# The opening of a transformer block with backward pass: loads in order of need, scores behind the first K and Q, other K and V spread between attention steps

## The chip, the core and the metric

The kernel runs on one core of a Trainium2 chip. A core has five engines that run side by side: TensorE (PE, matmuls), VectorE (DVE), ScalarE (ACT, activations such as exp), GpSimd (POOL) and SyncE (SP, which issues DMA transfers). They synchronise by semaphores. On-chip memory is SBUF (128 partitions); matmuls write to PSUM. The metric is device time in microseconds, the median over runs. A profile is of one execution, so its span can differ a little from the median.

## What is computed

The forward pass of a conditioned transformer block (2048 tokens, width 512, 32 heads of 16, MLP of 1792) and the gradients of all its inputs. The change touches the very beginning: layer norm, modulation by `c`, and Q, K and V of the attention.

```python
mod = (silu(c) @ w_mod).reshape(1, 6, 1, -1)         # sa, ca, ga, sb, cb, gb
h = layernorm(x) * (1 + ca) + sa
q, k, v = split(h @ wqkv)                            # 32 heads of 16
p = softmax(einsum('bhqd,bhkd->bhqk', q, k) * 16 ** -0.5)
x = x + ga * (einsum('bhqk,bhkd->bhqd', p, v) @ wo)
h = layernorm(x) * (1 + cb) + sb
x = x + gb * (relu(h @ w1 + b1) ** 2 @ w2 + b2)
# outputs: x, and the gradients of x, wqkv, wo, w1, b1, w2, b2, c, w_mod for a given grad_out
```

## The kernel before

Heads are worked in quads (`g`, 8 of them), queries in chunks of 512 (`qc`, 4 of them). A *unit* is one chunk of queries with a pair of heads: 64 units, each of `ST` = 16 steps `kb`, one for each block of 128 keys. A step makes scores for two heads (128x1024 in PSUM), ScalarE takes their exponential, and two or more steps later TensorE multiplies it with V ("PV"). In the order of TensorE and SyncE the program's order holds (`manual_schedule`); the other engines' instructions may be reordered when the program is built. So the exponentials of all 64 x 16 = 1024 steps form one stream on ScalarE, and other work ("background": Q and K of later quads, the MLP of earlier chunks) is woven between the steps of TensorE.

```python
KT = kp.tile([P, S], BF16, name="KTq")
first = self.gen_open(Vaug, KT, QTm, stp)
next(first)                                   # opening, first block of 512 tokens
for n, (qc, g, jp) in enumerate(order):       # 64 units
    ...
    for kb in range(ST):                      # 16 steps
        ...
        if n == 0 and kb % 4 == 0:
            next(first, None)                 # a further block of 512 tokens: at kb = 0, 4, 8 (12: the end)
        stt = stp.tile([P, 2, 512], F32, name="st")
        for a in range(2):
            nc.tensor.matmul(stt[:, a, :], lhsT=KT[:, kb * P:(kb + 1) * P], rhs=QTm[2 * jp + a][:], ...)
        pu = pup.tile([P, 2, 512], BF16, name="pu")
        nc.scalar.activation(pu[:], stt[:], ACT.Exp, scale=self.scale)
        ...                                   # PV of earlier steps
        rate = (1.14 if qc else 1.2) if n or kb > 11 else 0
        if rate:
            bg.step(rate)                     # background work
```

`gen_open` is the opening. `DT` = 4 (512 features in tiles of 128), `DH` = 16.

```python
for s4 in range(0, ST, 4):
    nc.sync.dma_start(x0[:, s4:s4 + 4, :], x_v[:, s4:s4 + 4, :])
for t in (1, 0, 2):                           # K, Q, V weights
    nc.scalar.dma_start(wq[:, :, t * D:(t + 1) * D], w_v[:, :, t * D:(t + 1) * D])
for t in (1, 0):                              # weights padded: each head's 16 columns in a field of 32
    nc.vector.memset(wpads[t][:], 0.0)
    for kt in range(DT):
        nc.scalar.copy(wpads[t][:, kt]..., wq[:, kt, t * D:(t + 1) * D]...)
nc.vector.memset(Vaug[:, :, :, DH:DH + 1], 1.0)
self.mod_cols(ps, (0, 1))                     # silu(c) @ w_mod for sa and ca: 32 small matmuls
...
for s4 in range(0, ST, 4):                    # a block: 4 tiles of 128 tokens
    for st in range(s4, s4 + 4):
        nc.vector.bn_stats(stats[:, st, :], x0[:, st, :])
        nc.vector.bn_aggr(mv[:, st, :], stats[:, st, :])
    nc.vector.tensor_scalar(ve[:, b], mv[:, b, 1], EPS, None, ALU.add)
    nc.gpsimd.tensor_tensor(self.rstd1[:, b], ve[:, b], self.mhalf[:], ALU.pow)
    nc.vector.scalar_tensor_tensor(nmr[:, b], ...)
    for st in range(s4, s4 + 4):              # xhat: odd tiles on VectorE, even ones on ScalarE
        ...
    tp = stp.tile([P, DT, 512], BF16, name="st")
    ...                                       # 16 transposes on TensorE
    for kt in range(DT):                      # xm1T = xhat^T * (1 + ca) + sa, VectorE and ScalarE in turn
        ...
    for _ in self.gen_fm(ps, 1, 0, s0, dst=KT[:, s0:s0 + 512]):
        pass                                  # K of quad 0
    if s4 == 0:
        for _ in self.gen_fm(ps, 0, 0, 0, masked=QTm):
            pass                              # Q of quad 0, chunk 0, and its masked copies
    for st in range(s4, s4 + 4):              # V: 4 matmuls a tile, evicted by ScalarE and VectorE in turn
        ...
    if s4 == 0:
        nc.gpsimd.dma_start(self.wmod[:, :, 2 * D:6 * D], wmod_v[:, :, 2 * D:6 * D])
        ...                                   # GpSimd memsets of vpads
    yield 0
```

`gen_fm` is four matmuls of 128x512 into a PSUM tile of the pool `ps` (two buffers, name `pps`), an eviction by VectorE, a store and a DMA transpose. The loads of `c` and of the first third of `w_mod` and the small chain silu(c) (VectorE, ScalarE and again VectorE) are in `phase0`, ahead of this.

Of the kernel before, what the change touches and what calls it, by code (L numbers as in the profile page):

```python
# [104 lines left out]
class K:  # L105
# [70 lines left out]
    def phase0(self):  # L176
# [19 lines left out]
        sb = self.open_pool("modp", bufs=1, side="right")  # L196
        cT_b = sb.tile([P, DT], BF16, name="cT_b")
        with nc.allow_non_contiguous_dma(reason="tiny column-layout load"):
            nc.sync.dma_start(cT_b[:], io["c"].rearrange("o (t p) -> p (o t)", p=P))
        wmod = self.wmod = sb.tile([P, DT, 6 * D], BF16, name="wmod")  # L200
        wmod_v = io["w_mod"].rearrange("(kt p) n -> p kt n", p=P)
        nc.scalar.dma_start(wmod[:, :, 0:2 * D], wmod_v[:, :, 0:2 * D])
        cT = sb.tile([P, DT], F32, name="cT")
        nc.vector.tensor_copy(cT[:], cT_b[:])
# [55 lines left out]
    def phase_fwd(self):  # L260
# [63 lines left out]
        next(first)  # L324
        for n, (qc, g, jp) in enumerate(order):
            if (qc, g, jp) == (1, 0, 0):
                bg.drain()
                self.close_qkv()
                self.open_mlp()
                bg.add(self.gen_weights())  # L330
            accb = accp.tile([P, 512], F32, name="accbank")
            acc = accb[:, 0:8 * (DH + 1)].rearrange("p (a s e) -> p a s e", a=2, s=4)
            self.cur_g = g
            for kb in range(ST):
                if kb == ST // 2 and n + 1 < len(order):
                    if n < 2 * NQ - 1 and jp == 1:
                        bg.until(g + 1)
                    load_q(*order[n + 1])
                    if jp == 1:
                        KTn = load_k(*order[n + 1][:2])  # L340
                if n == 0 and kb % 4 == 0:
                    next(first, None)
                stt = stp.tile([P, 2, 512], F32, name="st")
                for a in range(2):
                    nc.tensor.matmul(stt[:, a, :], lhsT=KT[:, kb * P:(kb + 1) * P], rhs=QTm[2 * jp + a][:],  # L345
                                     start=True, stop=True)
                pu = pup.tile([P, 2, 512], BF16, name="pu")
                nc.scalar.activation(pu[:], stt[:], ACT.Exp, scale=self.scale)  # L348
                u = (n, qc, g, jp, kb, acc, pu)
                now = n * ST + kb  # L350
                pend.extend((u, a, sub) for a in range(2) for sub in range(4))
                rate = (1.14 if qc else 1.2) if n or kb > 11 else 0
                room = int((SPAN - 2 - bg.plan(rate)) / PVT)
                while pend:
                    age = now - (pend[0][0][0] * ST + pend[0][0][4])
                    if age < 2 or (room <= 0 and age < 4):
                        break
                    pv(pend.pop(0))
                    room -= 1
                if rate:  # L360
                    bg.step(rate)
            if jp == 1 and n + 1 < len(order):
                if n < 2 * NQ - 1:
                    bg.until(-(g + 1))
                KT = KTn
# [13 lines left out]
    def gen_open(self, Vaug, KT, QTm, stp):  # L379
# [10 lines left out]
        wpads = self.wpads = [sb.tile([P, DT, NQ, P], BF16, name=f"wpad{t}") for t in range(2)]  # L390
        self.vpads = [sb.tile([P, NQ, 4, 32], BF16, name=f"vpad{i}") for i in range(2)]
        x0 = sa_.tile([P, ST, D], BF16, name="x0")
        x_v = io["A_x"][0].rearrange("(st p) d -> p st d", p=P)
        for s4 in range(0, ST, 4):
            nc.sync.dma_start(x0[:, s4:s4 + 4, :], x_v[:, s4:s4 + 4, :])
        w_v = io["A_wqkv"].rearrange("(kt p) n -> p kt n", p=P)
        for t in (1, 0, 2):
            nc.scalar.dma_start(wq[:, :, t * D:(t + 1) * D], w_v[:, :, t * D:(t + 1) * D])
        for t in (1, 0):
            nc.vector.memset(wpads[t][:], 0.0)  # L400
            for kt in range(DT):
                nc.scalar.copy(
                    wpads[t][:, kt].rearrange("p g (j e) -> p g j e", e=32)[:, :, :, 0:DH],
                    wq[:, kt, t * D:(t + 1) * D].rearrange("p (g j d) -> p g j d", j=4, d=DH))
        nc.vector.memset(Vaug[:, :, :, DH:DH + 1], 1.0)
        self.mod_cols(ps, (0, 1))
        xhat1 = sa_.tile([P, ST, D], BF16, name="xhat1")
# [4 lines left out]
        for s4 in range(0, ST, 4):  # L412
            b = slice(s4, s4 + 4)
            s0 = s4 * P
# [5 lines left out]
            nc.vector.scalar_tensor_tensor(nmr[:, b], mv[:, b, 0], -1.0, self.rstd1[:, b], ALU.mult, ALU.mult)  # L420
            for st in range(s4, s4 + 4):
                if st % 2:
                    nc.vector.tensor_scalar(xhat1[:, st, :], x0[:, st, :], mv[:, st, 0:1], self.rstd1[:, st:st + 1],
                                            ALU.subtract, ALU.mult)
                else:
                    nc.scalar.activation(xhat1[:, st, :], x0[:, st, :], ACT.Identity, bias=nmr[:, st:st + 1],
                                         scale=self.rstd1[:, st:st + 1])
            tp = stp.tile([P, DT, 512], BF16, name="st")
            for k in range(4):
                for kt in range(DT):  # L430
                    nc.tensor.transpose(tp[:, kt, k * P:(k + 1) * P], xhat1[:, s4 + k, kt * P:(kt + 1) * P], self.ident[:])
            for kt in range(DT):
                dst = xm1T[:, kt, s0:s0 + 512]
                if kt % 2:
                    nc.vector.tensor_scalar(dst, tp[:, kt, :], self.opcaT[:, kt:kt + 1], self.mod_col(0)[:, kt:kt + 1],
                                            ALU.mult, ALU.add)
                else:
                    nc.scalar.activation(dst, tp[:, kt, :], ACT.Identity, bias=self.mod_col(0)[:, kt:kt + 1],
                                         scale=self.opcaT[:, kt:kt + 1])
            for _ in self.gen_fm(ps, 1, 0, s0, dst=KT[:, s0:s0 + 512]):  # L440
                pass
            if s4 == 0:
                for _ in self.gen_fm(ps, 0, 0, 0, masked=QTm):
                    pass
            for st in range(s4, s4 + 4):
# [4 lines left out]
                (nc.vector.tensor_copy if st % 2 else nc.scalar.copy)(Vaug[:, st, :, 0:DH], pt[:].rearrange("p (h d) -> p h d", d=DH))  # L450
            nc.sync.dma_start(self.xhat1_d.rearrange("(st p) d -> p st d", p=P)[:, b, :], xhat1[:, b, :])
            if s4 == 0:
                wmod_v = io["w_mod"].rearrange("(kt p) n -> p kt n", p=P)
                nc.gpsimd.dma_start(self.wmod[:, :, 2 * D:6 * D], wmod_v[:, :, 2 * D:6 * D])
                for t in self.vpads:
                    nc.gpsimd.memset(t[:], 0.0)
                    nc.gpsimd.memset(t[:, :, :, DH:DH + 2], 1.0)
            yield 0
        self.close_pool("p1a")

# [4 lines left out]
    def gen_fm(self, ps, t, g, s0, dst=None, masked=None):  # L465
# [5 lines left out]
        for kt in range(DT):  # L471
            nc.tensor.matmul(pt[:], lhsT=self.wpads[t][:, kt, g, :], rhs=self.xm1T[:, kt, s0:s0 + 512],
# [1124 lines left out]
```

The softmax here doesn't subtract the row's maximum and nothing guards it: scores larger than these inputs give would overflow.

## Time and profile before

| | |
|---|---|
| time, median of 3 | 2691.65 us (2686.25 to 2698.53) |
| span of the profiled execution | 2680.6 us |
| busy: PE, PE weight loads | 2486.6 us (93%), 1229.1 us (46%) |
| busy: ACT, DVE, POOL | 2307.9 us (86%), 1764.2 us (66%), 393.4 us (15%) |
| first exponential starts, last one ends | 48.73 us, 1012.71 us |
| DMA | 439.59 MB, mean 164 GB/s |

How to read the lines of a profile: a group or a timeline line has a start and a duration in us, the engine (PEld is TensorE's weight load, SPq the issuing queue of SyncE), the line of the program, the operation, the tile written and the tiles read, shapes, a count (x4 means four in a row, merged), and in brackets how long the engine was idle before and what released it ("issue": no wait that the profile shows). A matmul's duration includes its latency, so matmuls in a row start closer together than they last. In a table of windows, each row is a stretch of time, with the busy time and count of each engine, the clock that TensorE was granted, the share of DMA engine time and the rate.

### The profile page before, as it was taken

The page shows a single profiled execution, that of the slowest core. Times are in us where ns is not written, and L with a number is a line of the kernel's source. Part 1 is how long each engine was busy: PE and PEld are TensorE (multiplying, and loading weights), DVE is VectorE, ACT ScalarE, POOL GpSimd, SP SyncE. Part 2 cuts the span into 40 slices and gives each one's busy share as a digit, 9 for nine tenths or more (in the row PEclk, how much of TensorE's full clock was granted, in tenths as well). Part 3 has the DMA queues.
Part 4 walks back from the last instruction along what each step waited for, and adds up shares of the span by engine and source line. Part 5 has one row for each costly group of instructions (what it writes and reads, how often), then busy time and mean ns, then how long its engine had stood idle before and what let it go on. Part 6 is the DMA issues. An engine that isn't in the chain of part 4 may idle for free.

```text
span 2680.6 us, 76637 instructions
## 1 busy us (share of the span) xinstructions
PE 2486.6 (93%) x30980; PEld 1229.1 (46%) x31210; DVE 1764.2 (66%) x3650; ACT 2307.9 (86%) x3728; POOL 393.4 (15%) x661
## 2 busy tenths in 40 slices
PE   5999999999999998898999999999999999999997
PEld 2555555555555554653443444444444434443443
DVE  4222222423423344656999999999999999999857
ACT  4999999999999995326999999999999999999823
POOL 2234531320221131351000000000000000000032
PEclk9999999999999999999999999999999999999999
DMA  4367752440441244999999999999999999999997
GB/s 146 91 146 160 175 121 69 114 110 21 124 115 54 86 98 122 222 224 173 201 196 198 199 196 198 200 202 202 194 199 200 203 198 200 196 197 209 208 217 175
DMA packets 1198027, 439.59 MB, mean 164 GB/s; under 512 B 1135430, under 2 KB 1159496, under 8 KB 1197672
## 3 DMA queue, kind: packets, MB, share of 16 engines
q1 hardware_dynamic: 1165608, 342.70, 70.4%
q0 software_dynamic: 29952, 89.36, 11.5%
q8 instruction: 244, 4.00, 0.6%
q10 hardware_dynamic: 2112, 2.62, 0.3%
q14 instruction: 111, 0.91, 0.1%
HBM read 83.30 MB, written 67.11 MB: 56 GB/s over the span
## 4 chain that ended last, share of the span: by engine, by line
PE 29%; DMA 24%; issue 3%; ACT 2%; DVE 1%; POOL 0%; SPq 0%; POOLq 0%; ACTq 0%; DVEq 0%
DMA dsT<-ds 22%; PE st L1315 11%; PE acckv L1217 6%; PE accq L1239 5%; ACT pu L1319 1%; PE dps L848 1%; PE g3ps L1421 1%; PE dp L1260 1%; DMA a_blk<-aT_d 1%; PE dxhps L1396 1%; PE st L1279 1%; PE dps L797 1%; PE st L1228 1%; DMA wo<-in_A_wo_dram 0%; PE g3ps L1408 0%
## 5 line engine op out<-in xcount | busy, mean ns | idle before, releaser
L1262 DVE TENSOR_TENSOR ds<-dp,pu 128x512 bf16<-128x512 f32 x2048 | 1243.0, 679 | 62.5 <-PE dp L1260 53.9
L1319 ACT ACTIVATE pu<-st 128x512 bf16<-128x512 f32 x2048 | 1082.8, 613 | 104.7 <-PE dp L1260 67.5
L348 ACT ACTIVATE pu<-st 128x1024 bf16<-128x1024 f32 x1024 | 943.0, 1072 | 6.7 <-PE st L345 4.7
L345 PE MATMUL st<-QTm,KTq 128*128 128x512 bf16 x1923 | 579.4, 377 | 31.1 <-ACT pu L348 9.6
L309 PEld LDWEIGHTS <-pu 128*128 128x128 bf16 x8192 | 347.4, 96 | 235.4 <-ACT pu L348 0.4
L1239 PEld LDWEIGHTS <-dsT 128*128 128x128 bf16 x8192 | 244.9, 96 | 273.7 <-issue 205.3
L309 PE MATMUL accbank<-Vaug,pu 128*128 128x17 bf16 x8192 | 357.7, 171 | 7.1 <-ACT pu L348 0.3
L1260 PE MATMUL dp<-m,dOTq 64*128 64x512 bf16 x1024 | 339.5, 383 | 0.0
L1260 PE MATMUL dp<-m,q 64*128 64x512 bf16 x1024 | 338.7, 384 | 0.7 <-DVE g2w L854 0.7
L1315 PE MATMUL st<-m,q 64*128 64x512 bf16 x1024 | 321.3, 383 | 8.4 <-ACT pu L1319 6.5
L1315 PE MATMUL st<-m,QTq 64*128 64x512 bf16 x1024 | 320.6, 383 | 6.3 <-ACT pu L1319 4.5
L345 PEld LDWEIGHTS <-KTq 128*128 128x128 bf16 x2048 | 194.1, 96 | 187.0 <-issue 132.6
L1370 POOL DMA_DIRECT2D O_tm<-O_d x2 | 1.8, 912 | 1323.1 <-PE accq L1239 1323.0
L1239 PE MATMUL accq<-q,dsT 128*128 128x16 bf16 x4096 | 150.8, 170 | 31.4 <-DMA dsT<-ds 31.3
L1239 PE MATMUL accq<-Kg,dsT 128*128 128x16 bf16 x4096 | 148.8, 170 | 28.9 <-DMA dsT<-ds 28.4
L1217 PE MATMUL acckv<-ds,Qg 128*16 128x512 bf16 x1024 | 155.3, 383 | 0.3 <-DVE ds L1262 0.2
L1217 PE MATMUL acckv<-pu,q 128*16 128x512 bf16 x1024 | 155.3, 383 | 0.0
L1217 PE MATMUL acckv<-ds,q 128*16 128x512 bf16 x1024 | 155.3, 384 | 0.0
L1217 PE MATMUL acckv<-pu,dOg 128*16 128x512 bf16 x1024 | 154.9, 383 | 0.0
L1280 ACT COPY dsT<-st 128x512 bf16<-128x512 bf16 x256 | 152.5, 596 | 1.5 <-PE st L1279 1.4
L316 DVE RECIPROCAL rl<-accbank 128x4 f32<-128x4 f32 x128 | 22.9, 179 | 163.2 <-PE accbank L309 163.2
L1315 PEld LDWEIGHTS <-q 64*128 64x128 bf16 x1024 | 58.1, 94 | 123.1 <-issue 104.2
(313 smaller groups left out, 2627.7 us busy)
## 6 DMA issues: line engine op xcount, KB each, us to landing
KTq<-KTq_d POOLq DMA_DIRECT2D x24, 512.0 KB, 3.6
duT_d<-auT POOLq DMA_DIRECT2D x4, 1792.0 KB, 8.8
aT_d<-rT POOLq DMA_DIRECT2D x4, 1792.0 KB, 13.7
KTq_d<-KTq SPq DMA_DIRECT2D x32, 128.0 KB, 1.8
QTq_d<-ev_fm SPq DMA_DIRECT2D x32, 128.0 KB, 2.0
VTq_d<-vT POOLq DMA_DIRECT2D x4, 1024.0 KB, 6.2
O_d<-O POOLq DMA_DIRECT2D x4, 1024.0 KB, 5.4
m<-KTq_d SPq DMA_DIRECT2D x32, 128.0 KB, 3.6
```

The lines of the kernel that those rows point to most:

```text
L309: nc.tensor.matmul(acc[:, a, sub, :], lhsT=pu[:, a, sub * P:(sub + 1) * P], rhs=Vaug[:, kb, h, :], start=(kb == 0 and a == 0 and sub == 0) ...
L345: nc.tensor.matmul(stt[:, a, :], lhsT=KT[:, kb * P:(kb + 1) * P], rhs=QTm[2 * jp + a][:], start=True, stop=True)
L348: nc.scalar.activation(pu[:], stt[:], ACT.Exp, scale=self.scale)
L797: nc.tensor.matmul(g4[:, kt, :], lhsT=xh2[:, st, kt * P:(kt + 1) * P], rhs=du[:, st, :], start=(st == 0), stop=(st == ST - 1))
L848: nc.tensor.matmul(pt[:], lhsT=a[:, st, :], rhs=g_tm[:, st, :], start=(st == 0), stop=(st == ST - 1))
L1217: nc.tensor.matmul(acckv[r:r + DH, :], lhsT=T[n][:, ib, col:col + DH], rhs=src[:, a, :], start=(ib == 0), stop=(ib == ST - 1))
L1239: nc.tensor.matmul(accq[:, ib, a, :], lhsT=dsT[:, (i * 2 + a) * 4 + sub, :], rhs=T["K"][:, 4 * c + sub, col:col + DH], start=(c == 0 and i ...
L1260: nc.tensor.matmul(dp[:], lhsT=T["dOT"][rd, ib * P:(ib + 1) * P], rhs=masked["VT"][2 * jp + a][rd, 512 * c:512 * (c + 1)], start=True, sto ...
L1262: nc.vector.tensor_tensor(dsg[:, i, a], dp[:], pu[:, a, :], ALU.mult)
L1280: nc.scalar.copy(dsT[:, 0:4, :], tp[:])
L1315: nc.tensor.matmul(stt[:], lhsT=T["QT"][rs, q], rhs=masked["KT"][2 * jp + a][rs, c0:c0 + 512], start=True, stop=True)
L1319: nc.scalar.activation(pu[:, a, :], stt[:], ACT.Exp, scale=self.scale)
```

## The change

The change rewrites the opening with the aim that scores start directly behind the first K and Q, that loads arrive in the order in which they are needed, that the rest of K and V is woven between the steps of the first unit, and that GpSimd doesn't work on SBUF while VectorE is needed.

- Loads: all from SyncE's queue, in order of need. `c` is loaded as four rows and transposed by TensorE.
- Padding: a small padded weight of quad 0 (`wpad0`) for K and Q is made first, by ScalarE; the padding of the other quads goes to GpSimd, behind the first Q.
- TensorE multiplies ones twice ten times ahead of the first block (results unused).
- The norm of a block is a function of its own; apart from the first block all its xhat are made by VectorE. Transposes go through the pool `pps` in halves instead of through a scores buffer.
- V of block 0 is no longer ahead of the first scores. In the first unit, each step takes so many pieces of the opening (`opening` divided over the four steps of a block), behind its scores.
- The large remaining part of w_mod is loaded last, from SyncE instead of GpSimd; GpSimd's memsets of `vpads` come behind the first Q.

The core of the diff (cuts marked with `...`):

```diff
-        nc.sync.dma_start(cT_b[:], io["c"].rearrange("o (t p) -> p (o t)", p=P))
-        nc.scalar.dma_start(wmod[:, :, 0:2 * D], wmod_v[:, :, 0:2 * D])
+        nc.sync.dma_start(self.c_row[:], io["c"].rearrange("o (t p) -> (o t) p", p=P))
+    def silu_c(self, ps):
+        pt = ps.tile([P, 1024], BF16, name="pps")
+        nc.tensor.transpose(pt[:, :DT], self.c_row[:], self.ident[:DT, :DT])
 ...
+        opening = [9 + DT + DT * 4] * (SC - 1) + [4 * DT + 1]
 ...
-                if n == 0 and kb % 4 == 0:
-                    next(first, None)
 ...                                            (behind the scores and the exponential of the step)
+                if n == 0:
+                    left = opening[kb // 4]
+                    take = -(-left // (4 - kb % 4))
+                    opening[kb // 4] -= take
+                    for _ in range(take):
+                        next(first)
 ...
+        load_x(0)
+        nc.sync.dma_start(self.wmod[:, :, 0:2 * D], wmod_v[:, :, 0:2 * D])
+        load_w(1)
+        load_w(0)
+        if SC > 1:
+            load_x(4)
+        load_w(2)
+        for s4 in range(8, ST, 4):
+            load_x(s4)
+        nc.sync.dma_start(self.wmod[:, :, 2 * D:6 * D], wmod_v[:, :, 2 * D:6 * D])
+        self.silu_c(ps)
+        warm = ps.tile([P, 512], F32, name="pps")
+        for _ in range(10):
+            nc.tensor.matmul(warm[:], lhsT=self.ones_b[:], rhs=QTm[0][:], start=True, stop=True)
         for t in (1, 0):
-            nc.vector.memset(wpads[t][:], 0.0)
-            for kt in range(DT):
-                nc.scalar.copy(wpads[t][:, kt]..., wq[:, kt, t * D:(t + 1) * D]...)
+            nc.vector.memset(self.wpad0[t][:], 0.0)
         nc.vector.memset(Vaug[:, :, :, DH:DH + 1], 1.0)
+        nc.vector.memset(wpads[1][:], 0.0)
+        nc.scalar.memzero(wpads[0][:])
+        for t in (1, 0):
+            nc.scalar.copy(self.wpad0[t][:]..., wq[:, :, t * D:t * D + 4 * DH]...)
         self.mod_cols(ps, (0, 1))
+        ...                                     (again ten matmuls with ones)
 ...
+        norm(0)
+        for _ in turn(0):
+            pass
+        for _ in self.gen_fm(ps, 1, 0, 0, dst=KT[:, 0:512]):
+            pass
+        for _ in self.gen_fm(ps, 0, 0, 0, masked=QTm):
+            pass
+        ...                                     (GpSimd: padding of the other quads, memsets of vpads)
+        yield 0
+        for s4 in range(4, ST, 4):
+            norm(s4)
+            yield from turn(s4)
+            yield from values(s4 - 4, s4 - 2)
+            yield from self.gen_fm(ps, 1, 0, s4 * P, dst=KT[:, s4 * P:s4 * P + 512])
             yield 0
+            yield from values(s4 - 2, s4)
+        yield from values(ST - 4, ST)
```

## Prediction

> **What bounds the kernel now.** I first cut the span into stretches: up to the first attention exponential, up to the last gap in their stream, the stream itself, the turn into the backward pass, the backward pass.
>
> ```profile
> core 0: us, PE busy (x) PEld busy (x) DVE busy (x) ACT busy (x) POOL busy (x), PEclk, DMA share, GB/s
> 0.00:48.73 48.73, 20.43 (x109) 9.21 (x112) 27.84 (x82) 18.11 (x28) 14.43 (x32) 0.93 0.56 183
> 48.73:72.83 24.10, 19.00 (x143) 9.44 (x144) 6.40 (x11) 13.01 (x17) 1.88 (x4) 0.93 0.23 71
> 72.83:1012.71 939.88, 900.87 (x11053) 511.82 (x11254) 276.91 (x791) 935.41 (x1016) 258.54 (x454) 1.00 0.43 105
> 1012.71:1230.00 217.29, 184.29 (x1523) 112.37 (x1534) 110.85 (x456) 69.14 (x158) 79.72 (x113) 0.95 0.90 196
> ```
>
> From 72.83 us to 1012.71 us ScalarE is busy 935.41 of 939.88 us with 1016 exponentials of 128x1024: 0.925 us each, and nothing else. That stage is bound by ScalarE, so its end is fixed by when the stream starts and how full the first steps are. Before 72.83 us ScalarE is busy 31.1 us only. The gain can lie only there. The timeline of ScalarE shows the gaps:
>
> ```profile
> 48.73 3.77 ACT L348 ACTIVATE pu<-st 128x1024 bf16<-128x1024 f32 x4 [0.71 <-PE st L345]
> 52.73 0.78 ACT L438 ACTIVATE xm1T<-st,modT,opcaT 128x512 bf16<-128x512 bf16 x1 [0.23 <-PE st L431]
> 56.80 0.59 ACT L450 CAST Vaug<-pps 128x512 bf16<-128x512 f32 x1 [1.91 <-PE pps L448]
> 59.98 3.77 ACT L348 ACTIVATE pu<-st 128x1024 bf16<-128x1024 f32 x4 [0.79 <-PE st L345]
> 72.83 37.31 ACT L348 ACTIVATE pu<-st 128x1024 bf16<-128x1024 f32 x40 [0.77 <-PE st L345]
> ```
>
> Four exponentials run, then a whole block of opening work (transposes, K, V) stands in TensorE's order before the next four. The first unit's sixteenth exponential ends at 72.83 + 8 x 0.925 = 80.2 us.
>
> Why the first one waits until 48.73 us is seen in the timelines of VectorE, GpSimd, TensorE and the DMA issues:
>
> ```profile
> 1.25 10.41 SPq L395 DMA_DIRECT2D x<-in_A_x_dram  x4
> 11.09 0.12 DVE L208 RECIPROCAL sig<-sig 128x4 f32<-128x4 f32 x1
> 11.44 0.94 POOL L456 MEMSET vpad<- 128x1024 bf16 x1
> 12.90 0.48 DVE L405 MEMSET Vaug<- 128x512 bf16 x1 [1.69 <-issue]
> 15.59 0.69 DVE L416 BATCH_NORM_STATS2 stats<-x 128x6 f32<-128x512 bf16 x1 [2.20 <-DMA x<-in_A_x_dram]
> 20.23 0.15 DVE L418 TENSOR_SCALAR ve<-mv 128x4 f32<-128x4 f32 x1
> 30.66 1.91 PE L448 MATMUL pps<-wqkv,xm1T 128*128 128x512 bf16 x4
> 30.90 1.16 ACT L477 CAST QTm<-pps 32x512 bf16<-32x512 f32 x2 [3.03 <-PE pps L472]
> 32.84 3.02 PE L448 MATMUL pps<-wqkv,xm1T 128*128 128x512 bf16 x12 [0.27 <-DVE ev_fm L481]
> 35.80 1.04 POOL L419 TENSOR_TENSOR rstd<-ve,mhalf 128x4 f32<-128x4 f32 x1
> ```
>
> The first block of x is used only at 15.59 us, after a 2.20 us wait on its load, though it was the first large load of its queue: 6.8 MB come in together. The masked Q is ready at 30.90 + 1.16 = 32.06 us, and the first K at 29.9 us. So scores could start at 32 us; they start at 48.10 because eight V tiles and the whole second block stand ahead.
>
> **What the Trainium skill says.** "DMA: Bandwidth & Descriptors", section "Issuing engines are not separate DMA queues", says that transfers issued from different engines run on the same 16 DMA engines and interleave. The trace agrees: x, w_mod (two queues) and w_qkv share some 350 to 400 GB/s until 22 us, and x took 14.3 to 19.6 us from issue to landing.
>
> "TensorE: Matmul & The Clock Gate", section "Part 1: The HAM clock gate", says that an idle array runs at half clock until it has been busy for about 3.4 us. The trace agrees: four 128x512 matmuls take 1.91 us at 30.66 us, twelve take 3.02 us from 32.84 us; start to start about 0.43 against 0.22 to 0.25 us.
>
> "GPSIMD Engine Reference", section "1. Specifications", says that GpSimd shares its SBUF interfaces with VectorE, with contention in some forms of VectorE instruction. The trace is in line with it but doesn't prove it: VectorE's memset at 12.90 us follows 1.69 us of idling that no wait explains, beside a GpSimd memset of 0.94 us.
>
> **The change part by part.**
>
> *Loads.* All go on one queue in order of need: c, x block 0 (0.52 MB), a third of w_mod (1.05 MB), K and Q weights (0.52 MB each), x block 1, V weights, the rest. Data starts to move at about 2.5 us. At 350 GB/s, with 1.5 us for the end of a transfer (my estimate from the rates above), x 0 lands near 6 us, w_mod near 8.5, K weights near 10, Q weights near 11.5. bn_stats can begin some 9 us earlier than at 15.59.
>
> *Padding of weights.* Eight ScalarE copies (0.61 us each, 4.4 us busy) become two small ones for quad 0, plus one clearing of 128x4096 on ScalarE, which I take as 1.8 us by VectorE's same memset (1.76 us). The rest of the padding goes to GpSimd, needed only from the twelfth step on. VectorE keeps one 1.76 us memset, Vaug's 0.48 us and two small ones. GpSimd's memsets move behind the first Q.
>
> *Path to the first score.* VectorE from 6 us: four bn_stats (4 x 0.66) and aggregates, about 3.2 us; the silu of c and memsets that fall in between, about 2.5 us: ve near 12 us instead of 20.23. Before, ve to masked Q took 11.8 us (20.23 to 32.06). Of this I take off about 2 us for full clock (8 matmuls at 0.43 to 0.58 us become 0.22; the twenty extra matmuls with ones are there for that) and 2 us for the norms of blocks 1 and 2, which VectorE now does later. So 12 + 8 = 20 us, and the first exponential starts at 20.5 us instead of 48.73.
>
> *The first unit.* The work of the other three blocks is the same but spread: about eight pieces after each pair of scores. For four steps, by durations of the kernel before: TensorE has 8 scores (1.7 us), 16 transposes (0.9), 4 K matmuls (0.9), 16 V matmuls (3.6) and 32 small PV matmuls (0.8; eight of them hold the array for 0.20 us in the timeline): 7.9 us. ScalarE has 4 x 0.925 + 2 x 0.78 + 2 x 0.59 = 6.4 us. VectorE has the norm of the next block (4 bn_stats 2.6, aggregates and small ones 0.8, four xhat now all here 1.5) and 2 x 0.54 + 3 x 0.69 of evictions: 8.1 us. So ScalarE doesn't bind in this unit; TensorE and VectorE do, with two PSUM buffers between them, and I add 1.5 us of waiting per group of four: 9.5 us. The last group has only 16 V matmuls: 6.1 + 0.7 = 7 us. Sum: 3 x 9.5 + 7 = 35.5 us.
>
> *Sum.* The sixteenth exponential ends at 20.5 + 35.5 = 56 us instead of 80.2: 24 us earlier. From there 1008 exponentials at 0.925 us follow as before, and the turn and the backward pass (1668 us from 1012.71 us on) only shift, since neither reads anything that the change makes later. 2691.65 - 24 = 2667.5 us, 0.9% less.
>
> **Rivals.**
>
> *A. Spread work runs at ScalarE's pace.* If V's evictions hide and norms run ahead while VectorE waits, the unit takes 16 x 0.925 + 6 x 0.78 + 8 x 0.59 = 24 us; with a first exponential at 18 us the sixteenth ends at 42 us: gain 38 us, 2654 us. Against it: VectorE alone has some 37 us of work in the opening (sixteen bn_stats 10.5, norms and evictions by the rows above), which can't start before x lands at 6 us, so the last V is hardly evicted before 43 us.
>
> *B. A new wait takes the place of the old.* Seven tiles a block go through two PSUM buffers, each evicted behind an exponential of 0.92 us on ScalarE or behind a norm on VectorE; the transposes, which had buffers of the scores before, are among them. If each tile costs 1.7 us, a block takes 12 us, as in the kernel before (48.73 to 59.98 is 11.25 us, 59.98 to 72.83 is 12.85), the unit ends at 20.5 + 45 = 66 us and the gain is 14 us: 2677 us.
>
> *C. The single queue is slower.* A wait on weights that land at 15 us and ones matmuls standing ahead in TensorE's order would put the first score at 26 us: 2673 us. For it: the fourth x issue alone held its queue for 7.63 of the 10.41 us. Against it: what is first in the queue has no competitor now.
>
> *D. The gain is given back later.* Background work (other quads' Q and K, MLP) keeps its place against the exponentials, and TensorE is busy 900.87 of 939.88 us by modelled ends. If the stream lost 0.5% through it, 5 us would go. ScalarE idles 4.5 us of 940 in that stage, so I see no sign of it.
>
> **Range and chances.** Rivals A and B bound the size: 2654 to 2677 us. The three times of before spread over 12 us, so I widen to 2655 to 2683. A gain of over 2% (54 us) would need a sixteenth exponential at 26 us, which the 37 us of VectorE's work rules out, unless a later stage gains; a loss of over 2% needs something outside the opening.
>
> **What would show it.** In the changed profile: the first bn_stats near 6 us (loads), ve near 12 us, matmuls of the first K and Q at 0.22 us (clock), first exponential at 20.5 us, its sixteenth ending at 56 us, the next 1008 in 932 us, and from the last exponential to the end of the span 1668 us. An opening limited by PSUM buffers (B) would show TensorE waiting on evictions between steps; A would show ScalarE full from the start. I am wrong in kind if the sixteenth exponential comes earlier by the 24 us and the span does not follow, or if the stream's 0.925 us changes.

## The result, and the profile after

| | before | changed |
|---|---|---|
| time, median | 2693.03 us (2686.25 to 2698.53) | 2661.88 us (2658.34 to 2666.42) |
| ratio, 95% interval | | 0.9886 (0.9858 to 0.9915) |
| span of the profiled execution | 2680.6 us | 2661.3 us |
| first exponential starts | 48.73 us | 23.06 us |
| seventeenth exponential starts (first unit over) | 80.27 us | 61.72 us |
| last exponential ends | 1012.71 us | 990.58 us |

The table of windows of the changed kernel, cut at its own stages: to the first exponential, the first unit, the rest of the stream, the turn, the backward pass (this last cut lies 2.4 us behind the first exponential of the backward pass; the table of the experiments cuts there, and so has 215.0 and 1455.7 us).

```profile
core 0: us, PE busy (x) PEld busy (x) DVE busy (x) ACT busy (x) POOL busy (x), PEclk, DMA share, GB/s
0.00:23.06 23.06, 13.01 (x82) 5.92 (x84) 16.72 (x54) 8.23 (x11) 9.94 (x25) 0.85 0.93 324
23.06:61.70 38.64, 30.85 (x266) 16.38 (x269) 18.87 (x44) 24.10 (x30) 9.78 (x18) 1.00 0.35 86
61.70:990.58 928.88, 893.16 (x10977) 508.35 (x11179) 275.93 (x789) 926.49 (x1009) 260.18 (x454) 1.00 0.44 106
990.58:1208.05 217.47, 186.42 (x1532) 113.29 (x1543) 112.39 (x459) 71.32 (x162) 79.85 (x113) 0.93 0.89 196
1208.05:2661.30 1453.25, 1363.80 (x18152) 584.87 (x18160) 1340.94 (x2310) 1272.05 (x2508) 38.94 (x58) 0.98 1.09 198
```

The stream is as full of exponentials as before. What went is in front of it: 80.27 - 61.72 = 18.6 us. But the first unit alone takes 38.7 us, against 31.5 us before, and ScalarE is busy only 24.10 us of it. The start came 25.7 us forward and the unit gave 7.1 us of that back.

The timeline of ScalarE in the changed kernel:

```profile
9.64 0.40 ACT L428 COPY wpad<-wqkv 128x256 bf16<-128x256 bf16 x1 [5.70 <-DMA wqkv<-in_A_wqkv_dram]
9.95 0.20 ACT L210 ACTIVATE sig<-cT 128x4 f32<-128x4 f32 x1
23.06 1.02 ACT L351 ACTIVATE pu<-st 128x1024 bf16<-128x1024 f32 x1 [0.46 <-PE st L348]
32.27 1.02 ACT L351 ACTIVATE pu<-st 128x1024 bf16<-128x1024 f32 x1
42.55 1.02 ACT L351 ACTIVATE pu<-st 128x1024 bf16<-128x1024 f32 x1
52.08 1.02 ACT L351 ACTIVATE pu<-st 128x1024 bf16<-128x1024 f32 x1
61.72 38.01 ACT L351 ACTIVATE pu<-st 128x1024 bf16<-128x1024 f32 x41
```

Lines 3 to 7 are the first, fifth, ninth, thirteenth and seventeenth exponential: groups of four steps of 9.2, 10.3, 9.5 and 9.6 us. The first two lines show the sigmoid of silu(c) standing behind a copy that waits for the K weights.

The timelines of the other engines, at the places shown of before:

```profile
2.21 0.94 POOL L499 MEMSET vpad<- 128x1024 bf16 x1
4.51 0.48 DVE L424 MEMSET Vaug<- 128x512 bf16 x1 [1.71 <-issue]
7.18 0.68 DVE L443 BATCH_NORM_STATS2 stats<-x 128x6 f32<-128x512 bf16 x1
9.70 2.09 POOL L495 COPY wpad<-wqkv 128x448 bf16<-128x448 bf16 x4 [6.07 <-DMA wqkv<-in_A_wqkv_dram]
10.19 0.17 DVE L211 TENSOR_SCALAR sig<-sig 128x4 f32<-128x4 f32 x1 [2.33 <-ACT sig L210]
13.73 0.19 DVE L445 TENSOR_SCALAR ve<-mv 128x4 f32<-128x4 f32 x1
13.92 0.56 POOL L495 COPY wpad<-wqkv 128x448 bf16<-128x448 bf16 x1
14.52 1.06 POOL L446 TENSOR_TENSOR rstd<-ve,mhalf 128x4 f32<-128x4 f32 x1
17.39 0.95 PE L463 MATMUL pps<-ident,xhat 128*128 128x128 bf16 x14 [0.20 <-ACT xhat L451]
19.50 1.89 PE L524 MATMUL pps<-xm1T,wpad 128*128 128x512 bf16 x8 [1.16 <-DVE xm1T L470]
21.43 1.18 ACT L529 CAST QTm<-pps 32x512 bf16<-32x512 f32 x2 [2.04 <-PE pps L524]
```

The first statistics start at 7.18 us instead of 15.59 and no longer wait for x. But VectorE then stands 2.33 us in front of the sigmoid (fifth line). The eight matmuls of the first K and Q take 1.89 us, full clock. Q is ready at 22.6 us instead of 32.1.

One part of the change is not seen in the trace. GpSimd's work was to come behind the first Q and out of VectorE's way. The order in the program doesn't bind GpSimd: its memsets of vpad run from 0.88 us on, and the padding of the other quads from 9.70 to 14.48 us, beside VectorE's first statistics. The first power (rstd), which needs ve at 13.92 us, starts behind that padding at 14.52.

### The profile page after: what moved, and what is told of

It is laid out like the page before. It is cut to its first block, busy times and chain, and to the rows that moved or that the text cites. A ratio compares the mean times of both kernels' runs of the same rounds, so it can differ in the third digit from the quotient of the medians.

```text
span 2661.3 us, 76673 instructions
## 1 busy us (share of the span) xinstructions
PE 2487.2 (93%) x31000; PEld 1228.8 (46%) x31231; DVE 1764.9 (66%) x3654; ACT 2302.2 (87%) x3717; POOL 398.7 (15%) x668
## 5 line engine op out<-in xcount | busy, mean ns | idle before, releaser
L1314 DVE TENSOR_TENSOR ds<-dp,pu 128x512 bf16<-128x512 f32 x2048 | 1243.6, 681 | 63.2 <-PE dp L1312 55.8
L1312 PE MATMUL dp<-m,q 64*128 64x512 bf16 x1024 | 344.2, 389 | 0.7 <-DVE g2w L906 0.7
L1291 PE MATMUL accq<-Kg,dsT 128*128 128x16 bf16 x4096 | 149.8, 170 | 31.3 <-DMA dsT<-ds 31.0
L320 DVE RECIPROCAL rl<-accbank 128x4 f32<-128x4 f32 x128 | 22.9, 179 | 162.8 <-PE accbank L313 162.8
```

What stands on the lines that cost most here:

```text
L320: nc.vector.reciprocal(self.rl[:, st0:st0 + 4, h], acc[:, a, :, DH])
L1291: nc.tensor.matmul(accq[:, ib, a, :], lhsT=dsT[:, (i * 2 + a) * 4 + sub, :], rhs=T["K"][:, 4 * c + sub, col:col + DH], start=(c == 0 and i ...
L1312: nc.tensor.matmul(dp[:], lhsT=T["dOT"][rd, ib * P:(ib + 1) * P], rhs=masked["VT"][2 * jp + a][rd, 512 * c:512 * (c + 1)], start=True, sto ...
L1314: nc.vector.tensor_tensor(dsg[:, i, a], dp[:], pu[:, a, :], ALU.mult)
```

## The experiments

All times of one row come from one trace; "17th" is the start of the seventeenth exponential (for the kernel before: the ninth of a merged run of equal ones, at their mean step). "Stream" is from there to the end of the last exponential, "turn" from there to the first exponential of the backward pass, "back" the rest. Medians are of 4 to 14 runs.

| kernel | Q ready | first | 17th | stream | turn | back | median | ratio to before (95%) |
|---|---|---|---|---|---|---|---|---|
| before | 32.1 | 48.7 | 80.3 | 932.4 | 217.1 | 1450.8 | 2693.0 | |
| before, again | 31.3 | 47.8 | 79.4 | 938.4 | 213.0 | 1459.3 | 2692.3 | 1.0004 (0.9982 to 1.0027) |
| changed | 22.6 | 23.1 | 61.7 | 928.9 | 215.0 | 1455.7 | 2661.9 | 0.9886 (0.9858 to 0.9915) |
| changed, again | 22.9 | 23.4 | 62.2 | 928.9 | 220.8 | 1451.5 | 2661.4 | 0.9897 (0.9873 to 0.9921) |
| spread undone | 22.4 | 22.9 | 61.5 | 934.3 | 211.9 | 1451.0 | 2659.9 | 0.9885 (0.9860 to 0.9911) |
| queues undone | 36.7 | 37.4 | 76.1 | 929.8 | 214.6 | 1451.5 | 2673.6 | 0.9942 (0.9919 to 0.9965) |
| block ahead | 22.2 | 30.5 | 63.5 | 933.2 | 215.9 | 1453.8 | 2664.0 | 0.9922 (0.9895 to 0.9949) |
| silu first | 24.1 | 24.5 | 63.1 | 932.7 | 214.7 | 1453.2 | 2664.6 | 0.9919 (0.9894 to 0.9945) |
| third buffer | 22.2 | 22.7 | 58.1 | 934.2 | 219.2 | 1452.7 | 2655.0 | 0.9882 (0.9854 to 0.9909) |
| no background | 22.3 | 22.8 | 57.9 | 928.9 | 216.3 | 1451.5 | 2656.7 | 0.9894 (0.9868 to 0.9919) |
| no ones | 24.6 | 25.0 | 63.7 | 930.6 | 221.8 | 1463.2 | 2668.4 | 0.9921 (0.9895 to 0.9947) |
| combined | 25.1 | 25.5 | 55.8 | 936.4 | 212.0 | 1454.5 | 2661.9 | 0.9894 (0.9866 to 0.9922) |
| combined, queues of before | 30.9 | 31.6 | 62.9 | 929.9 | 205.3 | 1451.3 | 2660.8 | 0.9897 (0.9868 to 0.9927) |
| buffer and no background | 22.6 | 23.1 | 56.8 | 929.1 | 214.8 | 1448.9 | 2652.4 | 0.9880 (0.9859 to 0.9902) |

How to read it: the columns up to "17th" repeat within 0.9 us for one kernel (two rows each of before and changed). The three later ones vary by 10 to 17 us, whatever was changed ahead of them. So effects of a few microseconds in the opening are read from "17th", not from the medians.

### Both kernels again

The same two programs, without an edit.

> The kernel before once more, for its spread from run to run. If the whole gain lies in the opening, as the traces say (19 us), further runs of before lie near the profiled 2682 us; if the timed medians tell the truth (31 us), they lie at 2690 to 2695 us and the difference to the trace is in a stage that varies from run to run, the backward pass.

> The changed kernel once more. Theory 'opening only': 19 to 24 us below before. Rival 'something else gains too': 28 us or more below. In its trace the first exponential starts at 23 us and the sixteenth ends at 61.5 us, within 0.5 us; the backward pass may differ by several us.

Before came out at 2692.33 us with a spread of 20 us over 14 runs, the changed one at 2661.37 us. The ratio's interval is a gain of 21 to 34 us, the opening's own gain in the two new traces is 79.4 - 62.2 = 17.2 us. So the opening isn't all of it. Part of the rest is seen in ScalarE's waits in the stream of this trace of before:

```profile
ACT pu L348 <- PE accbank L309: 3.8, 1, 3.8
```

(who waits for whom, us in total, times, longest). One wait of 3.8 us near 324 us is in this trace and not in the first one of before; the same comes, 3.1 to 3.9 us long, in spread undone, block ahead, third buffer and combined, and is missing in the others. It comes and goes with no tie to the opening that the traces show. "Turn" and "back" vary too. The first trace of before is also of a quick execution: 2682.5 us, 10 us below the median; the second is of 2692.0 us.

The medians' difference (31 us) goes beyond the opening's by 12 to 14 us. Chance alone is an unlikely account of that: by the ratio column, all twelve rows with the change gain more than their seventeenth exponential came forward (from 80.3 us), by 4 to 12 us, against five sets of runs of before. The clock granted over the whole execution doesn't settle it: its mean was 0.985 in before, 0.987 in changed, again, and 0.984 in queues undone, which has the excess as well. No trace shows the stage where it arises; its cause stays open.

### Spread undone

```diff
-                    take = -(-left // (4 - kb % 4))
+                    take = left
```

> The changed kernel, but each further block of the opening is taken at once behind the first scores of four steps instead of being divided over them. Theory (scores keep flowing because K and V are spread): the groups of four steps take 11 to 12 us instead of 9.2 to 10.3, the sixteenth exponential ends 5 to 8 us later, and the time rises by as much. Rival (TensorE's work sets the first unit whatever its order): the unit keeps its 38 us and the time stays within 2 us.

ScalarE's timeline of this kernel:

```profile
22.88 1.02 ACT L351 ACTIVATE pu<-st 128x1024 bf16<-128x1024 f32 x1 [0.46 <-PE st L348]
30.83 3.78 ACT L351 ACTIVATE pu<-st 128x1024 bf16<-128x1024 f32 x4
41.21 3.77 ACT L351 ACTIVATE pu<-st 128x1024 bf16<-128x1024 f32 x4
51.64 3.77 ACT L351 ACTIVATE pu<-st 128x1024 bf16<-128x1024 f32 x4
58.80 3.77 ACT L351 ACTIVATE pu<-st 128x1024 bf16<-128x1024 f32 x4 [0.42 <-PE st L348]
```

The exponentials come in clumps again, one and then four at a time. But the unit lasts 38.7 us, as before the edit. The rival holds: spreading by itself is worth nothing here.

### Block ahead

```diff
+        for _ in range(opening[0]):
+            next(first)
+        opening[0] = 0
```

> The changed kernel, but the second block of the opening (its transposes, its K and the V of the first block) is taken ahead of the first scores, as the kernel before had it; the rest stays spread. Theory (scores directly behind the first K and Q bring the stream forward): the first exponential comes some 9 us later, at 32 us, and the sixteenth ends 8 us later, at 69 to 70 us; time up by 8 us. Rival (the opening is one chain of four blocks, and where the scores stand in it hardly counts): the first exponential comes as late, but the first four steps then run at 0.92 us each, so the sixteenth ends at 62 to 65 us and the time rises by 3 us at most.

```profile
30.45 4.70 ACT L354 ACTIVATE pu<-st 128x1024 bf16<-128x1024 f32 x5
63.53 2.88 ACT L354 ACTIVATE pu<-st 128x1024 bf16<-128x1024 f32 x3
```

ScalarE's timeline: the first exponential comes 7.4 us late, and then five run back to back (4.70 us). At the seventeenth only 1.8 us of the 7.4 are left. The rival holds again. An early first exponential is worth little while the blocks behind it still have to go through the same queue.

### Queues undone

```diff
-        load_w = lambda t: nc.sync.dma_start(wq[:, :, t * D:(t + 1) * D], ...)
+        load_w = lambda t: nc.scalar.dma_start(wq[:, :, t * D:(t + 1) * D], ...)
-        load_x(0)
-        nc.sync.dma_start(self.wmod[:, :, 0:2 * D], ...)
-        ...
+        nc.scalar.dma_start(self.wmod[:, :, 0:2 * D], wmod_v[:, :, 0:2 * D])
+        for s4 in range(0, ST, 4):
+            load_x(s4)
+        for t in (1, 0, 2):
+            load_w(t)
+        nc.gpsimd.dma_start(self.wmod[:, :, 2 * D:6 * D], wmod_v[:, :, 2 * D:6 * D])
```

> The changed kernel with the loads on the queues of before: x on SyncE's, a third of w_mod and then the w_qkv parts on ScalarE's, the rest of w_mod early from GpSimd. Theory (order of loads brings the first bn_stats forward): x block 0 comes at 14 to 15 us, ve at 19 to 20 us instead of 13.7, and the first exponential and the time 5 to 7 us later. Rival (VectorE's memsets and the silu chain hold the first norm anyway): under 2 us.

The first exponential came 14 us late, twice what was expected. The timelines show that this is more than the loads:

```profile
12.91 1.29 DVE L439 BATCH_NORM_STATS2 stats<-x 128x6 f32<-128x512 bf16 x2 [5.82 <-DMA x<-in_A_x_dram]
18.49 0.15 DVE L441 TENSOR_SCALAR ve<-mv 128x4 f32<-128x4 f32 x1
20.31 0.15 DVE L208 CAST cT<-pps 128x4 f32<-128x4 bf16 x1
```

VectorE's order isn't pinned. With other queues it put the silu chain (cT at 20.31 us) behind the statistics, so mod_cols, which stands ahead of the transposes in TensorE's order, was late as well. A second try with the order held came later, below.

### Silu first

```diff
-        nc.scalar.activation(sig[:], cT[:], ACT.Exp, scale=-1.0)
+        self.sig_i = nc.scalar.activation(sig[:], cT[:], ACT.Exp, scale=-1.0)
 ...
+            with tc.issue_after(self.sig_i.ins):
                 nc.scalar.copy(self.wpad0[t][:]..., wq[:, :, t * D:t * D + 4 * DH]...)
```

> The changed kernel with the exponential of silu(c) put ahead of the copies of the K and Q weights in ScalarE's order. Theory (VectorE stood 2.33 us before the second bn_stats behind a sigmoid that stood behind the load of the K weights): sigmoid at 7.4 us instead of 10, ve 2 to 2.4 us earlier, first and sixteenth exponential 2 us earlier, time down 2 us. Rival (w_mod or the K weights then hold the chain): ve earlier, the first exponential within 0.7 us of where it was.

```profile
7.77 0.16 DVE L211 TENSOR_SCALAR sig<-sig 128x4 f32<-128x4 f32 x1
12.28 0.69 DVE L444 BATCH_NORM_STATS2 stats<-x 128x6 f32<-128x512 bf16 x1 [2.14 <-DMA x<-in_A_x_dram]
13.39 0.18 DVE L446 TENSOR_SCALAR ve<-mv 128x4 f32<-128x4 f32 x1
17.03 1.67 PE L464 MATMUL pps<-ident,xhat 128*128 128x128 bf16 x14 [0.31 <-ACT xhat L452]
19.30 3.53 PE L525 MATMUL pps<-xm1T,wpad 128*128 128x512 bf16 x8 [0.59 <-DVE xm1T L471]
```

The sigmoid came 2.4 us early, as meant. Then VectorE waited 2.14 us for block 1 of x, whose first statistics stand ahead of ve of block 0. One wait took the place of the other, and ve gained 0.3 us. Worse, mod_cols and the ten matmuls with ones now ran 2.5 us earlier, TensorE idled 1.53 us before the transposes, and those and the first K and Q ran at half clock: 3.53 us instead of 1.89. Both theories miss: the seventeenth exponential came 1.4 us later.

### Third buffer

```diff
-        accp = self.open_pool("fwacc", bufs=2, space=PSUM)
+        acc2 = [self.open_pool(f"fwacc{i}", bufs=1, space=PSUM) for i in range(2)]
+        accp = Pools(*acc2)
+        self.third = acc2[0]
 ...                                 (in gen_open: every third tile of the opening from self.third)
-        ps = self.mps
+        ps = Three()
```

> The changed kernel with a third PSUM buffer for the opening's tiles: the accumulator bank of the second unit, idle until then. Theory (two buffers and their evictions hold the first unit): TensorE's waits on evictions, 10 us in the first unit, fall by half, the groups of four take about 8.3 us instead of 9.5, the sixteenth exponential ends 4 us earlier, the time falls by 4 us. Rival (TensorE's own work and VectorE's norms set it): under 1 us.

The unit fell from 38.7 to 35.4 us, the seventeenth exponential came 3.6 us earlier than in the changed kernel: the theory, near its size. TensorE's idle time in the unit fell from 7.8 us (38.64 - 30.85) to 3.8 (35.43 - 31.67, from the windows of that trace). The groups are not even (8.0, 11.5, 7.9, 8.0 us, from ScalarE's timeline): in the second one TensorE waits 1.9 us for VectorE's modulation and then does four K matmuls in 1.91 us, half clock.

### No background work in the first unit

```diff
-                rate = (1.14 if qc else 1.2) if n or kb > 11 else 0
+                rate = (1.14 if qc else 1.2) if n else 0
```

> The changed kernel without background work in steps 12 to 15 of the first unit. My prediction's last group left it out. Theory (the Q and K tiles of the next quad share the two PSUM buffers and cost the 2 us that the last group took over my 7): the last group takes 7 to 7.5 us instead of 9.2 and the sixteenth exponential ends 2 us earlier; the work comes back in the second unit, so the time falls by 0 to 2 us. Rival (V's own evictions hold the last group): the group stays above 8.5 us.

```profile
51.76 1.02 ACT L351 ACTIVATE pu<-st 128x1024 bf16<-128x1024 f32 x1
57.85 8.38 ACT L351 ACTIVATE pu<-st 128x1024 bf16<-128x1024 f32 x9
```

Thirteenth and seventeenth exponential: the last group takes 6.1 us instead of 9.6, the first three are as before (9.2, 10.3, 9.5). The stream is no longer for it (928.9 us), so the work held back cost nothing there.

### No ones

Both times ten matmuls with ones left out; nothing else reads them.

```diff
-        warm = ps.tile([P, 512], F32, name="pps")
-        for _ in range(10):
-            nc.tensor.matmul(warm[:], lhsT=self.ones_b[:], rhs=QTm[0][:], start=True, stop=True)
```

> The changed kernel without the twenty matmuls with ones. Theory (TensorE's clock in the opening is part of the gain: 8 matmuls of the first K and Q and what follows until the clock is granted run at 0.43 instead of 0.22 us): the first Q is ready 1.7 to 2 us later, the first unit takes 1 to 3 us longer, the sixteenth exponential ends 3 to 5 us later. Rival (the ones stand in the way as much as they help): within 1 us.

```profile
19.77 3.57 PE L518 MATMUL pps<-xm1T,wpad 128*128 128x512 bf16 x8 [0.59 <-DVE xm1T L464]
24.82 1.12 PE L457 MATMUL pps<-ident,xhat 128*128 128x128 bf16 x16
```

The first K and Q at half clock (1.7 us more for the eight matmuls), Q 2.0 us later; from the next transposes on (1.12 us for sixteen) the clock is full again, and the unit keeps its 38.7 us, where 1 to 3 us more were expected. So the ones are worth 2 us, and only on the path to the first score. Of the two tens only the second can have helped: in the changed kernel the first ended at 6.67 us, TensorE then idled 5.36 us, and the second began at half clock (six in 2.72 us from 12.88 us).

### Combined, and combined with the queues of before

The third buffer, no background, silu first, 22 instead of 10 ones at first, and:

```diff
+            with (tc.issue_after(self.ve_i.ins) if s4 else ExitStack()):
+                for st in range(s4, s4 + 4):          # statistics of block 1 on: behind ve of block 0
+                    ...
+        with tc.issue_after(self.pow_i.ins):          # GpSimd's padding and memsets behind the first power
+            ...
```

> The changed kernel with what the other runs point to: third PSUM buffer, no background work in the first unit, sigmoid ahead of the weight copies on ScalarE, block 1's statistics behind ve of block 0 on VectorE, GpSimd's padding and memsets behind the first power, 22 instead of 10 matmuls with ones ahead of mod_cols so that TensorE has no gap there. Sum: ve at 10.7 us instead of 13.7, Q at 19.5 instead of 22.6, the unit 33.5 us instead of 38.7, the seventeenth exponential at 53 to 55 us instead of 62; the time 7 to 8 us below the changed kernel. Rival (buffers and background overlap, and another wait comes up in front): 58 us, no better than the third buffer alone. By the way: if VectorE's idling of 1.7 us ahead of the memset of Vaug comes from GpSimd's memsets, it goes here; if it belongs to that memset, it stays.

The second kernel has the loads as in "queues undone" besides, and VectorE's first statistics held behind the silu chain.

> The same, but with the loads on the queues of the kernel before, and VectorE's order held (silu chain, then block 0, then the others), which the earlier run of this kind did not do: there the silu chain had slipped behind four other blocks' statistics. Theory (the loads alone bring x block 0 some 6 us forward): first statistics at 13 us instead of 7.2, ve at 17 to 18 us, Q and the seventeenth exponential 6 to 7 us later than in the combined kernel. Rival (all 14 us of the earlier run are the loads'): 12 us or more later.

Timelines of the combined kernel:

```profile
4.51 0.48 DVE L436 MEMSET Vaug<- 128x512 bf16 x1 [1.71 <-issue]
10.38 0.17 DVE L459 TENSOR_SCALAR ve<-mv 128x4 f32<-128x4 f32 x1
11.66 4.19 POOL L511 COPY wpad<-wqkv 128x448 bf16<-128x448 bf16 x8
12.59 0.69 DVE L457 BATCH_NORM_STATS2 stats<-x 128x6 f32<-128x512 bf16 x1 [2.03 <-DMA x<-in_A_x_dram]
13.65 1.28 DVE L469 TENSOR_SCALAR xhat<-x,mv,rstd 128x512 bf16<-128x512 bf16 x2
15.79 1.84 POOL L515 MEMSET vpad<- 128x1024 bf16 x2
16.11 0.21 DVE L234 COPY modT<-accbank 128x4 f32<-128x4 f32 x2
16.39 1.35 DVE L237 TENSOR_SCALAR opcaT<-modT 128x4 f32<-128x4 f32 x1
20.69 3.15 PE L540 MATMUL pps<-xm1T,wpad 128*128 128x512 bf16 x7 [1.43 <-DVE xm1T L485]
```

ve came at 10.38 us as summed, and the unit took 30.3 us, better than summed; TensorE is busy 29.45 us of it, so it is TensorE's own work that is left there. Between the two the gain was lost: Q was ready at 25.1 us instead of the hoped-for 19.5. The wait for block 1 of x, 2.03 us here, was still in front: the edit holds these statistics behind ve, and VectorE took the first of them at 12.59 us, ahead of block 0's xhat, though the power was done at 11.69. VectorE read modT only at 16.11 us, though mod_cols was over near 10.6; two xhat took 1.28 us and one addition of 128x4 took 1.35 us beside GpSimd's copies and memsets, where the changed kernel has 0.73 and 0.33 us; and by 20.69 us TensorE had idled itself to half clock again (3.15 us for seven). The seventeenth exponential came at 55.8 us, near the sum; the median, forecast 7 to 8 us below the changed kernel, is level with it.

With the queues of before in this kernel, the order of VectorE held:

```profile
12.53 1.29 DVE L453 BATCH_NORM_STATS2 stats<-x 128x6 f32<-128x512 bf16 x2 [1.73 <-DMA x<-in_A_x_dram]
15.45 0.17 DVE L455 TENSOR_SCALAR ve<-mv 128x4 f32<-128x4 f32 x1
```

ve is 5.1 us later than in the combined kernel, Q 5.8, the seventeenth exponential 7.1. That is what the order of loads is worth in this kernel, half of what the first try said. The medians of the two combined kernels don't show it (2661.9 and 2660.8 us): in these traces the stream and the turn, 13 us apart, hide it.

### Buffer and no background

The two edits of those names together, nothing else.

> The changed kernel with only the two things that shortened the first unit: the third PSUM buffer and no background work in the first unit; nothing is reordered ahead of the first score. Theory (the two act on different groups of steps and add): first exponential at 22.5 to 23.4 us as in the changed kernel, the unit 30 to 31 us instead of 38.7, the seventeenth exponential at 53 to 54 us, the time 5 to 9 us below the changed kernel. Rival (later stages vary by more, and background work held back has to be made up at the turn of the units): the seventeenth as early, but the time not below the changed kernel's.

The first exponential at 23.1 us, the unit 33.7 us: less than the two gains added (38.7 - 3.2 - 3.6 = 31.9), but 5.0 us less than the changed kernel's. The seventeenth comes at 56.8 us. The theory that the two act on different groups of steps is wrong: both edits shorten the last group, from 9.6 us to 8.0 by the buffer, to 6.1 without background work, and to 6.1 with both. The kernel's median is 2652.4 us (2646.7 to 2656.5), and before measured with it 2686.1, ratio 0.9880 (0.9859 to 0.9902). It beats the kernel before. It wasn't timed side by side with the changed kernel, whose intervals overlap its own; that it is 5 us better is shown by the opening of its trace, not by the times.

## Why the prediction was right, and where it was not

The time was predicted at 2667.5 us in a range of 2655 to 2683; it is 2661.9. The direction and the place were right: a gain below 2%, all that a trace ties to the change lies ahead of the seventeenth exponential, and ScalarE's stream only moved forward. The two terms of the sum were both too good, by 2.6 and 3.2 us, so the opening gave 18.6 us instead of 24; by it alone the time would have been near 2673 us. That the median came within 6 us of the number is luck: the rest is the excess behind the opening, for which the prediction has no term. By step:

- *Loads.* Predicted: x block 0 near 6 us, first statistics some 9 us earlier. Measured: statistics at 7.18 us, held by VectorE's own memset up to then, 8.4 us earlier. The K and Q weights were there at 9.6 and 11.1 us, predicted near 10 and 11.5. Right, though the 1.5 us that the prediction adds for the end of a transfer don't follow from the rates it names. Taken alone with the order held, in the combined kernel, the loads are worth 5.1 us at ve and 7.1 at the end of the opening.
- *Path to the first score*, "12 + 8 = 20 us, and the first exponential starts at 20.5 us". Measured 23.06. The term that failed is ve "near 12 us": it came at 13.73, because VectorE stood 2.33 us before a sigmoid that ScalarE had put behind the wait for the K weights. The silu-first kernel removed that wait and met the next one (block 1 of x), so the wait is shown, but the 2 us weren't there to be had by this edit alone. The 8 us from ve to the first Q were 8.9. Some 0.5 us of that is the first power's wait behind GpSimd's padding (14.52 us, with ve ready at 13.92; in the combined kernel, without padding in front, it started 0.08 us behind ve). The prediction had put GpSimd's work behind the first Q.
- *Full clock.* Predicted 2 us, measured 2.0 by leaving the ones out. Right.
- *First unit*, "3 x 9.5 + 7 = 35.5 us". The three groups measured 29.0 instead of 28.5. The last one was mis-sized: 9.6 instead of 7 us, since I left out the background work that starts at step 12. Without it the group takes 6.1 us.
- *Rival B*, the two buffers, was given as one way in which it could go; a third buffer takes 3.2 us off the unit, so they are part of the bound, as was allowed for (1.5 us a group). *Rival A* is out: ScalarE was 24.10 us busy in 38.64. *Rival C* too: with one queue the K weights land by 9.6 us. *Rival D* is out: the stream didn't lengthen.
- *What the change is named for* counts less than I had it. I wrote that scores could start at 32 us and start at 48; the sum rightly counted only the end of the unit. The runs say how little the start is worth: scores directly behind the first K and Q 1.8 us, spreading nothing.

What made the opening 18.6 us shorter, then? The two traces split it: ve came 6.5 us earlier, the way from ve to Q is 3.0 us shorter, and that from Q to the seventeenth exponential 9.1. By undoing: loads 7.1 (in the combined kernel; 14.3 in the changed one, where VectorE's order changed with them), ones 2.0, scores ahead 1.8, spreading 0. These came from kernels of two bases and need not add. With the smaller figure for the loads some 7 or 8 us are left, with the larger next to nothing. The timelines of ScalarE and TensorE in the kernel before offer a cause:

```profile
37.59 0.81 ACT L426 ACTIVATE xhat<-x,nmr,rstd 128x512 bf16<-128x512 bf16 x1 [3.37 <-DVE nmr L420]
38.77 0.81 ACT L426 ACTIVATE xhat<-x,nmr,rstd 128x512 bf16<-128x512 bf16 x1
39.49 0.77 ACT L438 ACTIVATE xm1T<-st,modT,opcaT 128x512 bf16<-128x512 bf16 x1
40.31 1.17 PE L472 MATMUL pps<-xm1T,wpad 128*128 128x512 bf16 x2 [3.55 <-ACT xm1T L438]
42.66 5.61 PE L448 MATMUL pps<-wqkv,xm1T 128*128 128x512 bf16 x15
```

There the xhat of the last block, waiting 3.37 us for its norm, stood in ScalarE's order ahead of block 1's modulation, and TensorE waited 3.55 us for that and ran at half clock behind it: fifteen V matmuls in 5.61 us, against 3.77 us for fifteen of the next block, at 55.74 us. That is about 5 us. The change moved those xhat to VectorE. It fits in place and roughly in size, but no run undid this part alone, so it stays argued. The part of the gain that is not in the opening (31 us by the medians, 18.6 by the opening) has no cause shown at all.

## What to carry to other kernels

When an opening is one chain of blocks through one queue and a few buffers, measure it by where the full stream begins, not by where the first result appears: moving the first score 7.4 us moved the stream 1.8. Order loads by need, and look at every in-order engine for a small operation on the path that stands behind one waiting for a later load; after removing such a wait, look for the next before counting the gain. Effects below what later stages vary by have to be read from the stage in the trace.

## What the runs showed of the hardware that was not expected

- VectorE's idling of 1.7 us goes with the memset of Vaug that follows it (512 elements a partition, 17 apart). It was 1.69 to 1.72 us in all fourteen traces, with GpSimd's memset of vpad beside it or, as in the combined kernel, with that moved to 15.8 us and GpSimd idle. My reading of it as contention was wrong. What looks like contention is seen elsewhere: beside GpSimd's padding an xhat pair took 1.28 instead of 0.73 us and an addition of 128x4 1.35 instead of 0.33. "GPSIMD Engine Reference" of the Trainium skill, section "1. Specifications", names shared SBUF interfaces, and contention with VectorE instructions in a 2-port mode or with two SBUF inputs. In both combined kernels that addition ended 0.11 us behind GpSimd's memsets of vpad (17.74 and 17.63 us; 22.81 and 22.70 us), as if held until they were done. This is co-occurrence, not an isolated test, and no run shows in which mode the two instructions ran.
- Keeping TensorE busy is no switch. "TensorE: Matmul & The Clock Gate" of the Trainium skill, section "Part 1: The HAM clock gate", says that the clock comes after some 3.4 us of sustained activity and that the window runs freely. In the changed kernel ten matmuls with ones from 12.9 us brought full clock by 17.4; in silu first the same ten from 10.4 to 14.8 us left the array at half clock at 17.0 us. A free-running window would allow both: by my estimate from that figure two such windows are 6.8 us, and the ones with the small matmuls ahead of them lasted 5.3 us in silu first. In the combined kernel full clock outlived an idle stretch of 1.8 us and was lost by 18.7 us, after further ones of 0.4, 0.5 and 1.7 us.
